# Whole loads of q and k and a new order of the first two batches in an attention and MLP kernel on one core

## The chip, the cores and the metric

The kernel runs on one core of one Trainium2 chip. The metric is the time of one execution in device microseconds. Three runs of the kernel before gave a median of 285.89 us (285.8 to 286.83). A difference of 1 us is at the edge of what single times can tell; the traces, which show each instruction's start, tell more. A "span" below is the time from the first to the last instruction of one execution; it is 1.8 to 1.9 us shorter than the time of the same run.

Engines: PE is TensorE, DVE is VectorE, ACT is ScalarE, POOL is GpSimd, SP is the engine whose queue issues nearly all the loads here.

## The reference, cut to what matters

```python
def _attn_ref(q, k, v):                 # each (8 batches, 8 heads, 576, 64), float32
    q_s = exp(q - max(q, -1));  q_s = q_s / sum(q_s, -1)      # softmax over the 64 columns
    k_s = exp(k - max(k, 2));   k_s = k_s / sum(k_s, 2)       # softmax over the 576 rows
    kv = einsum('bhsd,bhse->bhde', k_s, v)                    # 64x64 per head
    return einsum('bhsd,bhde->bhse', q_s, kv)

def _moe_ref(x, w_in, w_out, beta):     # x (4608, 512), w_in (512, 2048), w_out (2048, 512)
    h = x @ w_in
    g = h * sigmoid(beta * h)
    return g @ w_out
```

The attention's output, with the heads side by side, is x. The kernel's types are float32 at both ends and bfloat16 inside.

## The kernel before: the parts that matter

Each batch goes through two parts. The attention part makes `xT` (x transposed, four chunks of 128 rows). The MLP part makes 16 tiles `h` of 128x512 (4 matmuls each), ACT takes `tanh` of each, DVE makes `g`, and PE multiplies `g` by `w_out` into four accumulators (`mm_b`, 4 matmuls for each g). Behind batch 1 the two parts of neighbouring batches are interleaved evenly. The head, in which batch 0's attention waits for its loads and has no MLP work beside it, and the stretch in which batch 1's attention is threaded by hand between batch 0's MLP matmuls, are written out instruction by instruction. The change is in these two parts.

The helpers, cut:

```python
def load_kv(d, src, b, tag, pairs=None):            # batches 0 and 1: one load per head pair, 288 KB
    ...
    sv = src[b].rearrange("(j e) (p i) d -> (e p) j (i d)", e=2, i=RW)
    for j in range(HP) if pairs is None else pairs:
        nc.sync.dma_start(d[b][:, j, :], sv[:, j, :])

def kz_exp(b, j): nc.scalar.activation(ek[b][:, j, :], k_st[b][:, j, :], ACTF.Exp)
def vz_cast(b, j, eng, m=1, part=None): ...         # v to bfloat16; part 0 is 5 of 9 rows, part 1 the other 4
def q_exp(b, s): ...                                # ACT: exp of half s of q
def q_sum(b, s): ...                                # DVE: row sums and their reciprocals
def q_mul(b, s): ...                                # DVE: multiply by them; both inputs in SBUF
def tpe(b, j, tag): ...                             # PE: 4 transposes of q's pair j;  q_ev copies the result to SBUF
def kvz_mm(b, j, tag, n): ...                       # PE: 18 small matmuls, k^T v of head pair j
def kvz_norm(b, j, n): ...                          # DVE: divide by k's sums
def xpe(c, j, tag): ...                             # PE: one matmul, xT chunk j into PSUM; xev copies it to SBUF
def hpe(c, j, kts, tag): ...                        # PE: pieces kts of h tile j, each one matmul on xT chunk kt
def w_castk(blk, kt, eng): ...                      # weight piece to bfloat16
def tail_zero(t): ...                               # POOL memsets of the buffers for the sequences' last rows
def warm(n, tag): ...                               # n matmuls on zeros that nobody reads
```

The head's loads and order, with cuts:

```python
    load_q(0, 2, 0)                                  # half of q, 512 KB
    nc.sync.dma_start(beta_r[:], ...)                # 8 rows of 1 KB
    load_kv(k_st, k, 0, "k_st", [0])
    load_kv(v_st, v, 0, "v_st", [0])
    load_q(0, 2, 1)
    load_kv(k_st, k, 0, "k_st", [2])
    load_kv(k_st, k, 0, "k_st", [3])
    load_kv(v_st, v, 0, "v_st", [2])
    load_kv(k_st, k, 0, "k_st", [1])
    load_kv(v_st, v, 0, "v_st", [1])
    load_kv(v_st, v, 0, "v_st", [3])
    w_load("in", 0, 0)                               # then the weights, 256 or 512 KB each
    ...
    tail_zero(0)
    tail_zero(1)
    warm(18, tag="b0")
    q_exp(0, 0)
    kz_exp(0, 0)
    q_sum(0, 0)
    vz_cast(0, 0, A, part=1)
    vz_cast(0, 0, G, part=0)
    kvz_mm(0, 0, "acc3", 1)
    q_mul(0, 0)
    ...                                              # 15 more warm matmuls in the gaps, in fours
    xpe(0, 1, "b3")
    xpe(0, 2, "acc3")
    w_castk(0, 1, G)
    hpe(0, 3, [0], "b0")                             # the first MLP matmul
    ...
```

The softmax here doesn't subtract the row's maximum and nothing guards it: scores larger than these inputs give would overflow.

## Time and profile before

| what | before |
|---|---|
| time, median of 3 | 285.89 us |
| span of the trace | 283.9 us |
| PE busy | 278.1 us, 98% |
| PE works without a break from | 17.39 us |
| last eviction starts at | 280.73 us |
| first weight cast of block 0 starts at | 14.87 us |

The page's first part gives busy time, share of the span and instructions for each engine; its fourth part gives the chain of waits that ended last, by engine. These are the two lines of the kernel before:

```profile
PE 278.1 (98%) x1683; PEld 130.5 (46%) x1683; DVE 179.6 (63%) x285; ACT 164.4 (58%) x241; POOL 37.8 (13%) x59
...
PE 94%; DMA 2%; DVE 2%; SPq 0%; POOL 0%; issue 0%; ACT 0%; POOLq 0%
```

PE is the bound. The same chain in order of time (start, length, what) shows where it is not PE. From the kernel before, between 12 and 18 us:

```profile
13.39 1.21 DVE eq L240
14.60 0.09 DVE rk L301
...
15.64 0.24 DVE kvp L304
15.88 0.05 issue
15.92 0.60 PE x L370 x2
16.52 0.65 PE h L422 x3
17.17 0.22 PE x L370
17.39 0.65 PE h L422 x3
```

Up to 15.9 us the chain is DVE's: the multiply of q's second half (L240), then the normalisations (L301, L304). After that it is PE until the last eviction. So the time is the moment at which PE's unbroken stretch begins, plus PE's work, plus any hole in the stretch.

Lines of the timeline of the kernel before (start, length, engine, line, operation, tiles, count, and in brackets what ended the idle time before it):

```profile
4.52 1.06 ACT L223 ACTIVATE eq<-q_st 128x1024 bf16<-128x1024 f32 x1 [2.50 <-DMA q_st<-in_q_dram]
...
13.07 0.46 POOL L158 CAST va<-v_st 128x320 bf16<-128x320 f32 x1 [0.84 <-DMA v_st<-in_v_dram]
...
13.31 1.29 DVE L240 TENSOR_TENSOR eq<-eq,rq 128x1024 bf16<-128x1024 bf16 x1
...
13.84 1.08 POOL L158 CAST va<-v_st 128x320 bf16<-128x320 f32 x1 [0.30 <-DMA v_st<-in_v_dram]
...
14.87 2.28 POOL L158 CAST w_in_b<-w_in 128x512 bf16<-128x512 f32 x4
```

The first half of q lands at 4.5 us, the last v pair at 13.8. The four casts of the first weight block follow on POOL without a gap.

The view by stretches gives, for each stretch in us, its length, then busy time (and instruction count) of PE, PE's weight loads, DVE, ACT and POOL, then the granted PE clock, the DMA engines' mean share and what they moved in GB/s. The kernel before, 3 to 7 us:

```profile
3.00:4.00 1.00, 1.00 (x4) 0.33 (x3) 0.01 (x1) 0.00 (x0) 0.89 (x4) 1.00 1.05 322
4.00:5.00 1.00, 1.00 (x3) 0.30 (x2) 0.00 (x0) 0.48 (x1) 1.00 (x3) 1.00 1.06 283
5.00:6.00 1.00, 1.00 (x4) 0.45 (x3) 0.40 (x1) 0.57 (x1) 0.22 (x3) 1.00 0.91 296
6.00:7.00 1.00, 1.00 (x7) 0.41 (x6) 0.97 (x2) 0.68 (x1) 0.00 (x0) 1.00 0.98 309
```

The DMA engines are occupied nearly all the time (0.91 to 1.06) and move about 300 GB/s, where they move 388 to 402 from 8 to 14 us (in stretches of 2 us).

### The profile page before, as it was taken

Reading aid. Unit: us, or ns where it says so; the run is one execution under the profiler, and the core shown is the slowest. Engines: PE = TensorE matmul, PEld = TensorE weight load, DVE = VectorE, ACT = ScalarE, POOL = GpSimd, SP = SyncE. Lnnn points to the kernel's source line nnn. Section 1 sums busy time; section 2 is a strip of 40 time slices with the busy share of each in tenths; the row PEclk is TensorE's granted clock in tenths of the full one; section 3 lists DMA queues with packets and bytes.
Section 4 is the critical chain, followed back from the end, with each engine's and each line's share of the span. In section 5 each row is a group of like instructions: output and inputs, shape, how many; then the busy total and the mean of one; then the engine's idle time right before and its main releaser. Section 6 shows DMA issues by size and latency. Waiting matters only on the chain.

```text
span 283.9 us, 4325 instructions
## 1 busy us (share of the span) xinstructions
PE 278.1 (98%) x1683; PEld 130.5 (46%) x1683; DVE 179.6 (63%) x285; ACT 164.4 (58%) x241; POOL 37.8 (13%) x59
## 2 busy tenths in 40 slices
PE   8899999999999999999999999999999999999995
PEld 3454445444444444444444444444445444445543
DVE  4765777875478457855685568646964596454361
ACT  4557796953496448734773468355944564454451
POOL 6374241130030003000300030000200000000000
PEclk9999999999999999999999999999999999999999
DMA  7999999919930993089416942598344032105003
GB/s 218 388 382 388 390 392 322 285 30 279 259 153 2 255 297 149 3 200 315 152 41 151 305 155 93 100 229 228 150 82 142 1 148 54 22 0 148 2 0 148
DMA packets 54932, 50.09 MB, mean 176 GB/s; under 512 B 26360, under 2 KB 47104, under 8 KB 54912
## 3 DMA queue, kind: packets, MB, share of 16 engines
q1 hardware_dynamic: 54768, 49.69, 58.1%
q8 instruction: 13, 0.21, 0.3%
q10 hardware_dynamic: 144, 0.13, 0.1%
q14 instruction: 7, 0.06, 0.1%
HBM read 36.71 MB, written 9.44 MB: 163 GB/s over the span
## 4 chain that ended last, share of the span: by engine, by line
PE 94%; DMA 2%; DVE 2%; SPq 0%; POOL 0%; issue 0%; ACT 0%; POOLq 0%
PE h L422 44%; PE acc L470 43%; PE x L370 2%; DMA v_st<-in_v_dram 2%; PE kv L330 2%; PE acc L462 1%; PE kv L289 1%; DVE rq L234 0%; DVE eq L240 0%; PE tp L270 0%; PE x L374 0%; DVE kvp L304 0%; POOL va L158 0%; DVE qsT L158 0%; PE warm L543 0%
## 5 line engine op out<-in xcount | busy, mean ns | idle before, releaser
L432 ACT ACTIVATE th<-h,beta_t 128x512 bf16<-128x512 f32 x144 | 98.5, 687 | 93.4 <-PE h L422 91.6
L436 DVE SCALAR_TENSOR_TENSOR g<-th,h 128x512 bf16<-128x512 bf16 x144 | 98.1, 683 | 85.9 <-ACT th L432 84.1
L422 PE MATMUL h<-xT,w_in_b 128*128 128x512 bf16 x576 | 144.0, 379 | 0.0
L470 PE MATMUL acc<-w_out_b,g 128*128 128x512 bf16 x560 | 140.8, 379 | 0.0
L422 PEld LDWEIGHTS <-w_in_b 128*128 128x128 bf16 x576 | 55.5, 98 | 63.9
L470 PEld LDWEIGHTS <-g 128*128 128x128 bf16 x560 | 54.4, 98 | 65.3 <-DVE g L436 0.5
L158 POOL CAST va<-v_st 128x320 bf16<-128x320 f32 (+2 forms) x14 | 16.7, 1192 | 150.0 <-DMA v_st<-in_v_dram 150.0
L234 DVE TENSOR_REDUCE rq<-eq 128x16 f32<-128x1024 bf16 x18 | 21.9, 1217 | 4.9 <-ACT eq L223 4.9
L240 DVE TENSOR_TENSOR eq<-eq,rq 128x1024 bf16<-128x1024 bf16 x18 | 22.0, 1221 | 0.1
L223 ACT ACTIVATE eq<-q_st 128x1024 bf16<-128x1024 f32 x16 | 16.2, 1048 | 2.5 <-DMA q_st<-in_q_dram 2.5
L156 ACT CAST xT<-x 128x512 bf16<-128x512 f32 x17 | 9.9, 585 | 8.6 <-PE x L370 7.8
L158 DVE COPY o<-acc 128x512 f32<-128x512 f32 (+1 forms) x19 | 12.1, 670 | 3.5 <-PE acc L470 3.2
L156 ACT COPY o<-acc 128x512 f32<-128x512 f32 (+1 forms) x18 | 9.6, 576 | 6.3 <-PE acc L470 3.4
L158 DVE CAST xT<-x 128x512 bf16<-128x512 f32 x19 | 12.8, 681 | 0.1
L177 ACT ACTIVATE ek<-k_st 128x1024 bf16<-128x1024 f32 x12 | 12.6, 1047 | 0.0
L370 PE MATMUL x<-qsT,kvp 128*128 128x512 bf16 x32 | 11.8, 380 | 0.2
L543 PE MATMUL warm<-kvp 128*128 128x512 bf16 x33 | 10.3, 465 | 1.2 <-DVE kvp L627 1.2
L158 POOL CAST w_in_b<-w_in 128x512 bf16<-128x512 f32 (+1 forms) x11 | 6.9, 650 | 6.4 <-DMA w_in<-in_moe_w_in_dram 6.4
L543 PEld LDWEIGHTS <-kvp 128*128 128x128 bf16 x33 | 3.6, 116 | 6.4 <-issue 3.6
L170 ACT ACTIVATE ek<-k_st 128x576 bf16<-128x576 f32 x8 | 5.4, 684 | 1.5 <-DMA k_st<-in_k_dram 1.5
L330 PEld LDWEIGHTS <-ek 128*64 128x64 bf16 x192 | 4.1, 111 | 2.5 <-ACT th L432 2.5
L363 DVE TENSOR_TENSOR kvp<-kv,rk 64x256 bf16<-64x256 f32 x12 | 5.1, 422 | 0.3
(45 smaller groups left out, 86.2 us busy)
## 6 DMA issues: line engine op xcount, KB each, us to landing
out_dram<-o SPq DMA_DIRECT2D x14, 512.0 KB, 3.4
q_st<-in_q_dram SPq DMA_DIRECT2D x6, 1024.0 KB, 6.4
k_st<-in_k_dram SPq DMA_DIRECT2D x6, 1024.0 KB, 9.2
v_st<-in_v_dram SPq DMA_DIRECT2D x6, 1024.0 KB, 10.7
w_in<-in_moe_w_in_dram SPq DMA_DIRECT2D x6, 512.0 KB, 9.4
k_st<-in_k_dram SPq DMA_DIRECT2D x8, 288.0 KB, 7.3
v_st<-in_v_dram SPq DMA_DIRECT2D x8, 288.0 KB, 7.4
q_st<-in_q_dram SPq DMA_DIRECT2D x4, 512.0 KB, 9.0
```

The source lines that it names most:

```text
L156: eng.copy(dst, src)
L158: eng.tensor_copy(dst, src)
L177: nc.scalar.activation(ek[b][:, :, h, :].rearrange("p i h d -> p h i d"), k_st[b][:, h, 0 : R * D].rearrange("p h (i d) -> p h i d", i=R), ...
L223: nc.scalar.activation(eq[b][:, :, s * m : (s + 1) * m, :].rearrange("p i h d -> p h i d"), q_st[b][:, s * m : (s + 1) * m, :].rearrange(" ...
L234: nc.vector.tensor_reduce(rq[b][:, 0, :, h], eq[b][:, :, h, :], axis=AX.X, op=ALU.add)
L240: eng.tensor_tensor(eq[b][:, :, h, :], eq[b][:, :, h, :], rq[b][:, 1, :, h].unsqueeze(3).to_broadcast((P, R, m, D)), ALU.mult,)
L370: nc.tensor.matmul(t[:], kvp[:, c, j, :], qsT[c][:, :, j, :])
L422: nc.tensor.matmul(h[:], w_unit(j, kt), x_of(c)[:, kt, :], start=(kt == 0), stop=(kt == KT - 1),)
L432: nc.scalar.activation(th[:], h_of[c, j][:], ACTF.Tanh, scale=beta_t[:, j : j + 1])
L436: nc.vector.scalar_tensor_tensor(out=g[:], in0=th_of.pop((c, j))[:], scalar=1.0, in1=h_of[c, j][:], op0=ALU.add, op1=ALU.mult)
L470: nc.tensor.matmul(acc[st][:], g[:, ds(st * P, P)], w_out_b[:, j, :], start=(j == 0), stop=(j == NJ - 1),)
L543: nc.tensor.matmul(t[:], kvp[:, B - 1, 0, :], kvp[:, B - 1, :, :].rearrange("p j r -> p (j r)"))
```

## The change

Its intent is a head in which PE's stretch begins sooner: q and k of batch 0 come in one load each, v by pairs in the order 0, 1, 2, 3, and the order of all engines' work is laid out anew for that, as is the order of batch 1 behind it. The zeroing of the tails' buffers moves from the start to behind that work. The number of warm matmuls goes from 33 to 31; 13 of them now stand in one block in front of the first transposes, instead of 15 spread over the gaps. The banks are renamed to fit. The diff, cut to its core:

```diff
-    load_q(0, 2, 0)
-    nc.sync.dma_start(beta_r[:], ...)
-    load_kv(k_st, k, 0, "k_st", [0])        # and v 0, q half 1, k 2, k 3, v 2, k 1, v 1, v 3
+    load_q(0)
+    load_kv(k_st, k, 0, "k_st", whole=True)
+    load_kv(v_st, v, 0, "v_st", [0])
+    load_kv(v_st, v, 0, "v_st", [1])
+    nc.sync.dma_start(beta_r[:], ...)
+    load_kv(v_st, v, 0, "v_st", [2])
+    load_kv(v_st, v, 0, "v_st", [3])
     ...                                     # weights: block 0 in the order 0, 3, 1, 2
-    tail_zero(0)
-    tail_zero(1)
     warm(18, tag="b0")
     q_exp(0, 0)
+    q_sum(0, 0)
+    q_exp(0, 1)
+    q_mul(0, 0)
     kz_exp(0, 0)
+    kz_exp(0, 1)
+    q_sum(0, 1)
+    vz_cast(0, 0, G)
+    warm(13, tag="acc2")
+    tpe(0, 0, "acc3")
+    tpe(0, 1, "acc2")
+    q_ev(0, 0, A)
+    kvz_mm(0, 0, "acc1", 1)
+    vz_cast(0, 1, G)
     ...                                     # [cut]
+    vz_cast(0, 3, G, part=0)
+    vz_cast(0, 3, A, part=1)
+    kvz_mm(0, 2, "acc1", 2)
+    xev(0, 0, A)
+    kvz_mm(0, 3)
+    w_castk(0, 0, G)
     ...                                     # [cut]
+    hpe(0, 3, [0], "b0")                    # the first MLP matmul now stands in front of xpe(0, 1)
+    kvz_norm(0, 2, 2)                       # pairs 2 and 3 in one normalisation
+    xpe(0, 1, "acc3")
     ...                                     # [cut: batch 0's MLP and batch 1's attention in a new order]
+    tail_zero(0)
+    tail_zero(1)
```

More of the change, by code (lines that the diff above doesn't have):

```diff
@@ L109, with load_kv @@
     kv_st = {}
-    def load_kv(d, src, b, tag, pairs=None):
+    def load_kv(d, src, b, tag, pairs=None, whole=False):
         if (tag, b) not in kv_st:
@@ L117, in load_kv @@
             sv = src[b].rearrange("(j e) (p i) d -> (e p) j (i d)", e=2, i=RW)
+            if whole:
+                nc.sync.dma_start(d[b], sv)
+                return
             for j in range(HP) if pairs is None else pairs:
@@ L252, in q_xbar @@
         )
-    HB, AB = ["b3", "b2"], ["b0", "b1"]
+    HB, AB = ["b3", "b0"], ["b1", "b2"]
     turns = {"h": 0, "att": 0}
@@ L584, in beta_ev @@
         )
-    load_q(0, 2, 0)
+    load_q(0)
+    load_kv(k_st, k, 0, "k_st", whole=True)
+    load_kv(v_st, v, 0, "v_st", [0])
+    load_kv(v_st, v, 0, "v_st", [1])
     nc.sync.dma_start(beta_r[:], moe_beta.rearrange("(hh q) -> hh q", q=2 * P))
-    load_kv(k_st, k, 0, "k_st", [0])
-    load_kv(v_st, v, 0, "v_st", [0])
-    load_q(0, 2, 1)
-    load_kv(k_st, k, 0, "k_st", [2])
-    load_kv(k_st, k, 0, "k_st", [3])
     load_kv(v_st, v, 0, "v_st", [2])
-    load_kv(k_st, k, 0, "k_st", [1])
-    load_kv(v_st, v, 0, "v_st", [1])
     load_kv(v_st, v, 0, "v_st", [3])
     w_load("in", 0, 0)
+    w_load("in", 0, 3)
     w_load("in", 0, 1)
     w_load("in", 0, 2)
-    w_load("in", 0, 3)
     w_load("in", 1, 0)
@@ L607 @@
     w_load("out", 1)
+    load_kv(v_st, v, 1, "v_st", [0])
+    w_load("in", 3, 0)
+    w_load("in", 3, 1)
     load_q(1, 2, 0)
-    w_load("in", 3, 1)
-    w_load("in", 3, 0)
-    load_kv(k_st, k, 1, "k_st", [2])
     w_load("out", 2)
     load_q(1, 2, 1)
+    load_kv(v_st, v, 1, "v_st", [1])
     load_kv(k_st, k, 1, "k_st", [0])
-    load_kv(v_st, v, 1, "v_st", [2])
-    w_load("out", 3, 0)
-    w_load("out", 3, 1)
-    load_kv(v_st, v, 1, "v_st", [0])
-    load_kv(k_st, k, 1, "k_st", [1])
-    load_kv(v_st, v, 1, "v_st", [1])
-    load_kv(k_st, k, 1, "k_st", [3])
-    load_kv(v_st, v, 1, "v_st", [3])
+    load_kv(k_st, k, 1, "k_st", [1])
+    w_load("out", 3, 0)
+    load_kv(k_st, k, 1, "k_st", [3])
+    w_load("out", 3, 1)
+    load_kv(v_st, v, 1, "v_st", [3])
+    load_kv(k_st, k, 1, "k_st", [2])
+    load_kv(v_st, v, 1, "v_st", [2])
     load_q(2)
@@ L632 @@
     v_buf(1)
-    tail_zero(0)
-    tail_zero(1)
     warm(18, tag="b0")
     q_exp(0, 0)
+    q_sum(0, 0)
+    q_exp(0, 1)
+    q_mul(0, 0)
     kz_exp(0, 0)
-    q_sum(0, 0)
-    vz_cast(0, 0, A, part=1)
-    vz_cast(0, 0, G, part=0)
-    kvz_mm(0, 0, "acc3", 1)
-    q_mul(0, 0)
-    beta_pe("acc2")
-    beta_ev()
-    kvz_norm(0, 0)
-    q_exp(0, 1)
-    warm(3, tag="acc1")
-    tpe(0, 0, "acc2")
-    tpe(0, 1, "acc1")
-    q_ev(0, 0, V)
-    q_ev(0, 1, V)
-    kz_exp(0, 2)
-    warm(1, tag="acc0")
@@ L655 @@
-    xpe(0, 0, "acc3")
-    q_sum(0, 1)
-    kz_exp(0, 3)
-    vz_cast(0, 2, G)
-    xev(0, 0, V)
-    warm(8, tag="acc1")
-    kvz_mm(0, 2, "acc2", 1)
-    kz_exp(0, 1)
-    q_mul(0, 1)
-    vz_cast(0, 1, A, part=1)
-    vz_cast(0, 1, G, part=0)
-    warm(3, tag="acc1")
-    kvz_mm(0, 1, "acc3", 1)
-    kvz_norm(0, 2)
-    vz_cast(0, 3, A, part=1)
-    vz_cast(0, 3, G, part=0)
-    tpe(0, 2, "acc1")
-    tpe(0, 3, "acc0")
-    kvz_norm(0, 1)
-    q_ev(0, 2, A)
-    kvz_mm(0, 3, "acc2", 1)
-    w_castk(0, 0, G)
@@ L677 @@
-    q_ev(0, 3, A)
-    kvz_norm(0, 3)
-    xpe(0, 1, "b3")
-    xpe(0, 2, "acc3")
+    kz_exp(0, 1)
[7 more added lines that the diff above has]
+    vz_cast(0, 1, G)
+    kz_exp(0, 3)
+    beta_pe("acc0")
+    kvz_norm(0, 0)
+    kvz_mm(0, 1, "acc3", 1)
+    vz_cast(0, 2, G)
+    kz_exp(0, 2)
+    q_mul(0, 1)
+    xpe(0, 0, "b3")
+    beta_ev()
+    vz_cast(0, 3, G, part=0)
+    vz_cast(0, 3, A, part=1)
@@ L681 @@
+    kvz_mm(0, 2, "acc1", 2)
+    xev(0, 0, A)
+    kvz_mm(0, 3)
+    w_castk(0, 0, G)
+    q_ev(0, 1, A)
+    kvz_norm(0, 1)
+    tpe(0, 3, "acc0")
+    tpe(0, 2, "b3")
+    w_castk(0, 3, G)
+    q_ev(0, 3, A)
+    hpe(0, 3, [0], "b0")
+    kvz_norm(0, 2, 2)
+    xpe(0, 1, "acc3")
+    hpe(0, 2, [0], "b1")
+    q_ev(0, 2, A)
     w_castk(0, 1, G)
-    hpe(0, 3, [0], "b0")
+    hpe(0, 1, [0], "b2")
     xev(0, 1, V)
-    hpe(0, 0, [0], "b1")
-    hpe(0, 2, [0], "b2")
+    hpe(0, 0, [0], "acc0")
@@ L686 @@
+    xpe(0, 3, "acc2")
     w_castk(0, 2, G)
-    xpe(0, 3, "acc2")
-    xev(0, 2, V)
-    hpe(0, 1, [0], "acc0")
-    xev(0, 3, A)
+    xpe(0, 2, "acc1")
+    xev(0, 3, V)
+    hpe(0, 1, [1])
+    xev(0, 2, A)
     hpe(0, 0, [1])
-    w_castk(0, 3, G)
     hpe(0, 3, [1])
-    hpe(0, 1, [1])
-    hpe(0, 3, [2])
-    hpe(0, 3, [3])
-    hpe(0, 1, [2])
-    th_act(0, 3)
     hpe(0, 2, [1])
-    w_castk(1, 0, G)
     hpe(0, 2, [2])
     hpe(0, 2, [3])
-    w_castk(1, 1, A)
+    w_castk(1, 0, G)
     hpe(0, 0, [2])
-    g_dve(0, 3)
@@ L706 @@
-    hpe(0, 7, [0], "b3")
-    hpe(0, 0, [3])
-    th_act(0, 2)
-    hpe(0, 4, [0], "acc1")
-    w_castk(1, 2, G)
-    hpe(0, 4, [1])
-    th_act(0, 0)
-    hpe(0, 5, [0], "b0")
-    g_dve(0, 2)
+    th_act(0, 2)
+    hpe(0, 1, [2])
+    w_castk(1, 1, G)
+    hpe(0, 1, [3])
+    hpe(0, 5, [0], "b3")
+    th_act(0, 1)
+    hpe(0, 3, [2])
+    g_dve(0, 2)
+    hpe(0, 5, [1])
+    w_castk(1, 2, G)
+    hpe(0, 3, [3])
+    w_castk(1, 3, A)
+    hpe(0, 0, [3])
+    g_dve(0, 1)
+    hpe(0, 6, [0], "b1")
@@ L715 @@
+    hpe(0, 5, [2])
+    th_act(0, 3)
+    hpe(0, 5, [3])
+    hpe(0, 7, [0], "b2")
+    th_act(0, 0)
+    hpe(0, 6, [1])
+    g_dve(0, 3)
+    w_cast("out", 0, 0, G)
     hpe(0, 7, [1])
-    w_castk(1, 3, G)
-    hpe(0, 1, [3])
-    hpe(0, 4, [2])
+    hpe(0, 7, [2])
+    th_act(0, 5)
+    hpe(0, 6, [2])
     g_dve(0, 0)
-    th_act(0, 1)
-    hpe(0, 7, [2])
-    hpe(0, 4, [3])
-    hpe(0, 6, [0], "b2")
-    w_cast("out", 0, 0, G)
-    th_act(0, 4)
-    hpe(0, 6, [1])
-    g_dve(0, 1)
-    hpe(0, 6, [2])
@@ L729 @@
     hpe(0, 6, [3])
-    hpe(0, 5, [1])
-    g_dve(0, 4)
+    hpe(0, 7, [3])
+    g_dve(0, 5)
     th_act(0, 6)
-    hpe(0, 5, [2])
-    hpe(0, 5, [3])
-    hpe(0, 7, [3])
-    w_cast("out", 0, 1, A)
+    hpe(0, 4, [0], "b0")
+    w_cast("out", 0, 1, G)
     mm_b(0, 0)
+    th_act(0, 7)
     g_dve(0, 6)
     mm_b(0, 1)
-    th_act(0, 7)
+    g_dve(0, 7)
     w_castk(2, 0, G)
-    th_act(0, 5)
-    g_dve(0, 7)
+    mm_b(0, 2)
     w_castk(2, 1, G)
-    mm_b(0, 2)
-    g_dve(0, 5)
-    w_castk(2, 2, A)
+    mm_b(0, 3)
@@ L748 @@
+    w_castk(2, 2, G)
     w_castk(2, 3, G)
-    mm_b(0, 3)
-    hpe(0, 8, [0, 1, 2, 3], "b0")
-    hpe(0, 10, [0, 1, 2, 3], "b1")
-    th_act(0, 8)
-    w_cast("out", 1, 1, G)
-    w_cast("out", 1, 0, A)
-    hpe(0, 9, [0, 1, 2, 3], "b2")
-    g_dve(0, 8)
-    hpe(0, 11, [0, 1, 2, 3], "b0")
+    hpe(0, 4, [1])
+    hpe(0, 4, [2])
+    hpe(0, 4, [3])
+    hpe(0, 8, [0, 1, 2, 3], "b1")
+    th_act(0, 4)
+    hpe(0, 9, [0, 1, 2, 3], "b2")
+    g_dve(0, 4)
+    th_act(0, 8)
+    w_cast("out", 1, 0, A)
@@ L758 @@
+    hpe(0, 11, [0, 1, 2, 3], "b0")
+    g_dve(0, 8)
+    vz_cast(1, 0, G, part=0)
+    hpe(0, 10, [0, 1, 2, 3], "b1")
+    th_act(0, 9)
+    th_act(0, 11)
+    w_cast("in", 3, 0, G)
+    g_dve(0, 9)
+    mm_b(0, 4)
+    w_cast("out", 1, 1, A)
+    g_dve(0, 11)
+    mm_b(0, 5)
+    vz_cast(1, 0, A, part=1)
     th_act(0, 10)
+    mm_b(0, 6)
+    w_cast("in", 3, 1, A)
+    g_dve(0, 10)
+    mm_b(0, 7)
     q_exp(1, 0)
-    g_dve(0, 10)
-    mm_b(0, 4)
-    th_act(0, 9)
+    hpe(0, 13, [0, 1, 2, 3], "b0")
@@ L763 @@
     q_sum(1, 0)
-    mm_b(0, 5)
-    w_cast("in", 3, 1, A)
-    mm_b(0, 6)
-    th_act(0, 11)
-    g_dve(0, 9)
-    w_cast("in", 3, 0, G)
-    mm_b(0, 7)
-    q_mul(1, 0)
-    hpe(0, 12, [0, 1, 2, 3], "b1")
-    g_dve(0, 11)
-    tpe(1, 0, "b2")
-    th_act(0, 12)
-    hpe(0, 13, [0, 1, 2, 3], "b3")
-    q_ev(1, 0, V)
-    g_dve(0, 12)
-    hpe(0, 14, [0, 1, 2, 3], "b0")
-    th_act(0, 13)
-    w_cast("out", 2, 1, G)
-    w_cast("out", 2, 0, A)
-    tpe(1, 1, "b1")
-    g_dve(0, 13)
-    hpe(0, 15, [0, 1, 2, 3], "b2")
@@ L786 @@
-    th_act(0, 14)
-    mm_b(0, 8)
-    q_exp(1, 1)
-    g_dve(0, 14)
-    mm_b(0, 9)
-    vz_cast(1, 2, G)
-    kz_exp(1, 0)
-    q_sum(1, 1)
-    mm_b(0, 10)
-    q_ev(1, 1, A)
-    kz_exp(1, 2)
-    w_cast("out", 3, 0, G)
-    mm_b(0, 11)
-    th_act(0, 15)
-    q_mul(1, 1)
-    kvz_mm(1, 2, "b0", 1)
+    hpe(0, 12, [0, 1, 2, 3], "b1")
+    th_act(0, 13)
+    hpe(0, 14, [0, 1, 2, 3], "b2")
+    w_cast("out", 2, 0, A)
+    w_cast("out", 2, 1, G)
+    g_dve(0, 13)
+    hpe(0, 15, [0, 1, 2, 3], "b3")
@@ new lines @@
+    th_act(0, 12)
+    q_mul(1, 0)
+    q_exp(1, 1)
+    mm_b(0, 8)
+    g_dve(0, 12)
+    vz_cast(1, 1, G)
+    th_act(0, 14)
+    mm_b(0, 9)
+    q_sum(1, 1)
+    th_act(0, 15)
+    mm_b(0, 10)
+    kz_exp(1, 0)
+    g_dve(0, 15)
+    mm_b(0, 11)
+    kz_exp(1, 1)
+    q_mul(1, 1)
+    w_cast("out", 3, 0, G)
+    tpe(1, 0, "b0")
+    tpe(1, 1, "b1")
+    q_ev(1, 0, A)
+    kvz_mm(1, 0, "b3", 2)
+    g_dve(0, 14)
+    kvz_mm(1, 1)
+    q_ev(1, 1, A)
+    tpe(1, 3, "b0")
+    kz_exp(1, 3)
+    kvz_norm(1, 0, 2)
@@ L802 @@
     mm_b(0, 12)
     w_cast("out", 3, 1, A)
-    g_dve(0, 15)
-    vz_cast(1, 0, G, part=0)
     tpe(1, 2, "b1")
-    kvz_norm(1, 2)
-    vz_cast(1, 0, A, part=1)
-    mm_b(0, 13)
-    q_ev(1, 2, V)
-    kz_exp(1, 1)
-    kvz_mm(1, 0, "b0", 1)
-    vz_cast(1, 1, A, part=1)
-    vz_cast(1, 1, G, part=0)
-    xpe(1, 2, "b1")
-    kvz_norm(1, 0)
-    tpe(1, 3, "b2")
-    kvz_mm(1, 1, "b3", 1)
-    kz_exp(1, 3)
-    q_ev(1, 3, V)
-    mm_b(0, 14)
-    kvz_norm(1, 1)
-    vz_cast(1, 3, A, part=1)
-    vz_cast(1, 3, G, part=0)
@@ L825 @@
-    xpe(1, 0, "b0")
-    xev(1, 2, V)
-    xpe(1, 1, "b2")
-    kvz_mm(1, 3, "b3", 1)
-    xev(1, 1, A)
-    xev(1, 0, V)
-    mm_b(0, 15)
-    kvz_norm(1, 3)
-    hpe(1, 0, [0], "b0")
-    store(0, 0)
-    hpe(1, 1, [0], "b1")
-    xpe(1, 3, "b2")
-    hpe(1, 3, [0], "b3")
-    store(0, 1)
-    xev(1, 3, A)
-    hpe(1, 3, [1])
-    hpe(1, 0, [1])
+    xpe(1, 1, "b2")
+    vz_cast(1, 3, G, part=0)
+    q_ev(1, 2, V)
+    xpe(1, 0, "b3")
+    vz_cast(1, 3, A, part=1)
+    mm_b(0, 13)
+    xev(1, 1, V)
@@ L842 @@
+    q_ev(1, 3, A)
+    kz_exp(1, 2)
+    kvz_mm(1, 3, "b1", 1)
+    vz_cast(1, 2, G, part=0)
+    mm_b(0, 14)
+    vz_cast(1, 2, A, part=1)
+    kvz_norm(1, 3)
+    xev(1, 0, A)
+    kvz_mm(1, 2, "b0", 1)
+    mm_b(0, 15)
+    kvz_norm(1, 2)
+    xpe(1, 3, "b1")
+    store(0, 0)
+    xpe(1, 2, "b0")
+    xev(1, 3, V)
+    hpe(1, 0, [0], "b2")
+    hpe(1, 0, [1])
+    xev(1, 2, A)
+    hpe(1, 2, [0], "b3")
+    store(0, 1)
+    hpe(1, 2, [1])
+    hpe(1, 1, [0], "b1")
     hpe(1, 0, [2])
@@ L849 @@
     hpe(1, 1, [3])
+    hpe(1, 2, [2])
+    th_act(1, 1)
+    hpe(1, 2, [3])
+    g_dve(1, 0)
+    hpe(1, 3, [0], "b0")
+    hpe(1, 3, [1])
+    th_act(1, 2)
     hpe(1, 3, [2])
+    g_dve(1, 1)
     hpe(1, 3, [3])
-    th_act(1, 1)
-    g_dve(1, 0)
-    hpe(1, 2, [0], "b2")
-    hpe(1, 2, [1])
+    mm_b(1, 0)
     th_act(1, 3)
-    hpe(1, 2, [2])
-    g_dve(1, 1)
-    hpe(1, 2, [3])
-    mm_b(1, 0)
-    th_act(1, 2)
+    g_dve(1, 2)
+    mm_b(1, 1)
     g_dve(1, 3)
-    mm_b(1, 1)
-    g_dve(1, 2)
+    tail_zero(0)
+    tail_zero(1)
     def side(n, u):
```

## The prediction

> **What bounds the kernel now.** TensorE. The page's first part has PE busy 278.1 of 283.9 us (98%); the chain of waits that ended last is 94% PE, 2% DMA, 2% DVE. From 17.39 us to the last eviction (280.73 us) that chain is PE without a break, each 512-column matmul starting 0.216 us after the one before. So only two things can change the time: when the unbroken stretch begins, and whether the new order tears a hole in it later. Useful PE work is the same; 2 of 33 warm-up matmuls, mere filling, go.
>
> **The head before.** By the timeline: first half of q lands at 4.5 us, k pair 0 at 6.3, v pair 0 at 7.8, the last v pair at 13.8; the four pieces of the first weight block are cast back to back by POOL from 14.87 to 17.15. By half-microsecond stretches, DMA's share is near 1 from 2.5 us on, with about 300 GB/s until 7.5 us and 390 after: bytes, not issue, set landings. The last steps before 17.39 are DVE's: multiply of q's second half until 14.6, three normalisations, the xT copies.
>
> **What the change does.**
> - Whole loads move no fewer bytes. Landings, counted as cumulative bytes plus the lag seen (0.9 to 2 us): q whole at about 7, k whole 10.8, v pairs 11.5, 12.3, 13.0, 13.8, weight pieces from 14.5 every 0.7 us. So q's first exp starts about 2.5 us later (before: 4.52), and the last v and the weights land as before.
> - DVE: the two q sums (1.47 each) and multiplies (1.2) run 8.3 to 14.55 with one normalisation between; evictions of qT and xT go to ACT (0.58 each); pairs 2 and 3 share one normalisation. That takes about 2 us off the end of DVE's chain.
> - PE takes the first weight piece against xT chunk 0 four times (from about 15.4 us) where before it waited until 15.9.
> - Zeroing of the tails, 3.6 us of POOL (1.67 to 5.28), moves to about 45 us, where POOL idles 10.4 us before batch 2's v cast. Before, POOL idled 2.6 us after it: worth nothing by itself.
>
> **How much is on the path.** Adding trace durations along these chains, the state that before reached at 17.39 comes at about 16.8. Gain 0.6 us (0.2%). Behind it, slack is small at g(1) freeing the bank for h7 (about 20.3), w_out 0 (about 22), w_in 2 and 3 (26, 33), batch 1's last v (45); I allow 0.1 us of new holes. Time 285.4 us, range 284.4 to 286.7. Faster by over 2%: 0.02; within 2%: 0.96; slower: 0.02.
>
> **What would show it.** q's exp starting at 6.5 to 7.5 us; last v landing within 0.3 us of 13.8; the first h matmul at 15.2 to 15.7 and PE unbroken from 16.6 to 17.1; PE idle after that under 0.3 us; POOL zeroing at 45 to 49 us delaying nobody.
>
> **What would make it wrong.** [...] (warm-up matmuls 0.43 us apart until 5.86 us, then 0.216). With fewer fillers PE is about half busy from 10.3 to 15.4 us; if the clock drops, the first h matmuls take twice as long and I lose 1 to 2 us. Else: whole loads landing later than counted, or weights arriving late.

The spacings in brackets behind the mark, 0.43 and then 0.216 us, are that trace's own, and "twice as long" is worked out from them. The sum: 285.9 less 0.6 plus 0.1 is 285.4 us, and the 1 to 2 us for a falling clock, the author's estimate, stood outside it.

## The result, and the profile after

| what | before | after |
|---|---|---|
| time, median of 4 runs | 285.86 us | 284.97 us (284.71 to 285.07) |
| span of the trace | 283.9 us | 282.9 us |
| q's first exp starts | 4.52 us | 6.51 us |
| last v pair in use from | 13.80 us | 12.56 us |
| first weight cast starts | 14.87 us | 13.82 us |
| last eviction starts | 280.73 us | 279.61 us |

The ratio is 0.996, with a 95% interval of 0.9937 to 0.9982. The change is 0.4% faster, inside the 2% that count as "the same".

The two lines of the page after:

```profile
PE 275.2 (97%) x1653; PEld 130.1 (46%) x1681; DVE 176.5 (62%) x274; ACT 164.9 (58%) x243; POOL 39.6 (14%) x60
...
PE 93%; DMA 3%; SPq 1%; POOL 1%; issue 1%; ACT 0%
```

(Some matmul records are missing: 1653 of 1681.) The chain in order of time after the change, from 4 to 18 us:

```profile
3.99 8.52 DMA v_st<-in_v_dram
12.51 0.05 issue
12.56 1.31 POOL va L161
13.88 1.13 POOL w_in_b L161 x2
15.00 0.01 issue
15.01 0.38 PE x L373
15.39 0.65 PE h L425 x3
16.04 0.43 PE x L373 x2
16.47 1.73 PE h L425 x8
```

DVE is gone from the chain. It is now a load of v, POOL's cast of it, two of POOL's weight casts, then PE. Timeline lines that answer to those of before:

```profile
6.51 2.00 ACT L226 ACTIVATE eq<-q_st 128x1024 bf16<-128x1024 f32 x2 [4.49 <-DMA q_st<-in_q_dram]
...
12.33 1.23 DVE L243 TENSOR_TENSOR eq<-eq,rq 128x1024 bf16<-128x1024 bf16 x1
...
12.56 1.31 POOL L161 CAST va<-v_st 128x320 bf16<-128x320 f32 x1
...
13.82 2.29 POOL L161 CAST w_in_b<-w_in 128x512 bf16<-128x512 f32 x4
...
16.30 5.65 PE L425 MATMUL h<-xT,w_in_b 128*128 128x512 bf16 x25
```

And the stretches from 3 to 7 us after:

```profile
3.00:4.00 1.00, 1.00 (x4) 0.32 (x3) 0.01 (x1) 0.00 (x0) 0.00 (x0) 1.00 0.98 299
4.00:5.00 1.00, 1.00 (x5) 0.35 (x4) 0.00 (x0) 0.00 (x0) 0.00 (x0) 1.00 1.08 384
5.00:6.00 1.00, 1.00 (x6) 0.48 (x5) 0.00 (x0) 0.00 (x0) 0.00 (x0) 1.00 1.05 361
6.00:7.00 1.00, 1.00 (x7) 0.46 (x5) 0.00 (x0) 0.49 (x1) 0.00 (x0) 1.00 1.04 396
```

Three things are to be seen. From 3 to 7 us the DMA engines deliver more (mean of the four stretches 360 GB/s, before 302); counted from 0 to 12 us the difference is small (298 against 288), because the changed kernel moves less before 3 us. POOL's cast of the last v pair takes 1.31 us, although the same shape took 0.46 us at 13.07 in the kernel before; it ends 0.31 us after DVE's multiply that began just ahead of it. This is not new: the kernel before shows the same for its last pair (1.08 us, to 0.32 us after the multiply), but there DVE's chain ended later and it cost nothing. And PE reaches the old state sooner. At 17.39 the kernel before had all of batch 0's attention and 3 h matmuls behind it; the new one has that and one h matmul more at 16.47 (the first of the four has no record; its weight load is at 14.74), so the same state at about 16.25. That is 1.14 us sooner. Of this 1.12 us are left at the last eviction (280.73 less 279.61).

### The profile page after: what moved, and what is told of

The parts are those of the page before. It is cut to its first block, busy times and chain, and to the rows that moved or that the text cites. A ratio compares the mean times of both kernels' runs of the same rounds, so it can differ in the third digit from the quotient of the medians.

```text
span 282.9 us, 4278 instructions
## 1 busy us (share of the span) xinstructions
PE 275.2 (97%) x1653; PEld 130.1 (46%) x1681; DVE 176.5 (62%) x274; ACT 164.9 (58%) x243; POOL 39.6 (14%) x60
## 4 chain that ended last, share of the span: by engine, by line
PE 93%; DMA 3%; SPq 1%; POOL 1%; issue 1%; ACT 0%
PE h L425 44%; PE acc L473 42%; DMA v_st<-in_v_dram 3%; PE x L373 2%; PE kv L333 2%; PE acc L465 1%; PE kv L292 1%; SPq L122 1%; POOL va L161 0%; POOL w_in_b L161 0%; PE tp L273 0%; PE x L377 0%; SPq L119 0%; SPq L593 0%; SPq L96 0%
## 5 line engine op out<-in xcount | busy, mean ns | idle before, releaser
L425 PE MATMUL h<-xT,w_in_b 128*128 128x512 bf16 x560 | 142.4, 379 | 1.0
L473 PE MATMUL acc<-w_out_b,g 128*128 128x512 bf16 x548 | 138.8, 379 | 0.5 <-issue 0.2
L161 POOL CAST va<-v_st 128x2048 bf16<-128x2048 f32 (+2 forms) x14 | 16.9, 1207 | 149.7 <-DMA v_st<-in_v_dram 149.4
L159 ACT CAST xT<-x 128x512 bf16<-128x512 f32 x18 | 10.6, 588 | 6.6 <-PE x L373 5.8
L546 PE MATMUL warm<-kvp 128*128 128x512 bf16 x31 | 8.5, 442 | 1.2 <-DVE kvp L626 1.2
L161 POOL CAST w_in_b<-w_in 128x512 bf16<-128x512 f32 (+1 forms) x12 | 7.5, 650 | 3.0 <-DMA w_in<-in_moe_w_in_dram 2.9
L161 POOL CAST w_out_b<-w_out 128x1024 bf16<-128x1024 f32 x4 | 5.0, 1248 | 7.5 <-DMA w_out<-in_moe_w_out_dram 7.5
```

The lines of the kernel that those rows point to most:

```text
L159: eng.copy(dst, src)
L161: eng.tensor_copy(dst, src)
L425: nc.tensor.matmul(h[:], w_unit(j, kt), x_of(c)[:, kt, :], start=(kt == 0), stop=(kt == KT - 1),)
L473: nc.tensor.matmul(acc[st][:], g[:, ds(st * P, P)], w_out_b[:, j, :], start=(j == 0), stop=(j == NJ - 1),)
L546: nc.tensor.matmul(t[:], kvp[:, B - 1, 0, :], kvp[:, B - 1, :, :].rearrange("p j r -> p (j r)"))
```

## The experiments

My theory after the result: the whole gain is the head's, through loads that arrive sooner and an order of work that suits them; the zeroing is worth nothing. Rivals: the zeroing slowed the loads (it stood exactly where they were slow); or batch 1's new order made the gain; or the head's order of work alone made it, whatever the loads. All kernels below gave correct results. "Span" is that of the one traced execution.

### Is it the zeroing?

`e1_before_zero_late` is the kernel before with

```diff
-    tail_zero(0)
-    tail_zero(1)
     warm(18, tag="b0")
     ...
     g_dve(1, 2)
+    tail_zero(0)
+    tail_zero(1)
```

> The kernel before with only the zeroing of the tails' buffers moved behind the head's work. Theory Z (POOL's memsets between 1.7 and 5.3 us slow the loads that run beside them): the last v pair lands near 12.6 us as in the changed kernel instead of 13.8, and the time falls by 0.4 us or more. Theory L (loads: fewer and larger ones land sooner) and theory O (the new order of the head's work): nothing moves, 285.8 us within 0.15, last v at 13.8, and the zeroing after 45 us delays nobody.

Measured: 285.7 us (284.98 to 286.08, 6 runs), ratio 0.9977 (0.9953 to 1.0001), span 283.9. POOL's cast of the last v pair began at 13.61, and the DMA engines moved 284 GB/s on average from 3 to 7 us.

`e2_after_zero_early` is the changed kernel with the two calls back in front of `warm(18)`.

> The changed kernel with the zeroing back at the start. Theory Z: DMA falls to about 300 GB/s until 5 us, q lands later than 6.5 us, the last v later than 12.6, and the time rises by 0.4 us or more to 285.4. Theories L and O: 284.9 us within 0.15, landings unchanged, because POOL has nothing else to do before the first v pair at 10.3.

Measured: 284.82 us (284.44 to 286.07), ratio 0.9956 (0.9933 to 0.998), span 283.0. q's exp began at 6.37, the last eviction at 279.63. Two of its stretches, with POOL zeroing (0.89 and 1.00 us busy) beside the loads:

```profile
3.00:4.00 1.00, 1.00 (x4) 0.33 (x3) 0.01 (x1) 0.00 (x0) 0.89 (x4) 1.00 1.05 375
4.00:5.00 1.00, 1.00 (x3) 0.30 (x2) 0.00 (x0) 0.00 (x0) 1.00 (x3) 1.00 1.06 366
```

So the zeroing costs nothing that these times can show in either place (at most about 0.1 us by `e1`'s last eviction, 280.64 against 280.73), and the loads are not seen to be slowed by it: in the two stretches above the DMA engines moved 375 and 366 GB/s beside it, where they moved 299 and 384 in the changed kernel without it, and q's exp began at 6.37 us against 6.51.

### Head or batch 1?

`e5_head_new_rest_old` has the new loads and order up to batch 0's h4, and from h8 on the old order, with banks b0, b1, b2 renamed b1, b2, b0 and the old order of the loads behind w_out 1. `e6_head_old_rest_new` is the reverse. Both zero late. Their edits are the diff above cut at one line:

```diff
     mm_b(0, 3)                              # and h4 where it is still open
     # e5: new above, old below;   e6: old above, new below
     hpe(0, 8, [0, 1, 2, 3], ...)
```

> The changed kernel's head (loads and order of batch 0 up to the end of h4) with the old loads and order from there to batch 1's g3, PSUM banks renamed to fit. If the whole gain is in the head: 285.0 us within 0.15 and PE's unbroken stretch starting near 16.5 us as in the changed kernel. The two traces show PE 0.2 us cheaper between 17 and 50 us in the new order (fewer switches from the small kv matmuls back to full ones); if that is real this run is 0.2 us slower than the changed kernel, 285.1 to 285.2.

> The old head (loads and order of batch 0) with the new loads and order of the rest, zeroing late. If the head makes the gain: 285.6 to 285.85 us, with the stretch starting at 17.4 as before and at most 0.2 us won behind it. If the rest makes it: 285.0.

Measured: `e5` 285.18 us (284.9 to 286.34), ratio 0.997 (0.9947 to 0.9992), span 283.3. `e6` 285.74 us (284.8 to 286.2), ratio 0.998 (0.9957 to 1.0003), span 283.7. The times of `e6` alone don't tell it from the kernel before. The traces do, if one takes the chain's times at two points: the first `mm_b` of batch 0 (three h pieces, 0.65 us, are added where the new head does them later), and the first h of batch 1 (0.43 us are taken off where two pieces were done before).

| kernel | first `mm_b` of batch 0 | first h of batch 1 | between them | last eviction |
|---|---|---|---|---|
| before | 23.65 | 48.18 | 24.53 | 280.73 |
| before, zeroing late (e1) | 23.50 | 48.09 | 24.59 | 280.64 |
| old head, new rest (e6) | 23.51 | 47.95 | 24.44 | 280.54 |
| new head, old rest (e5) | 22.86 | 47.39 | 24.53 | 279.94 |
| after | 22.60 | 47.05 | 24.45 | 279.61 |

Batch 1's new order is worth about 0.1 us: 24.44 and 24.45 against 24.53 to 24.59. The chain shows one source. The small kv matmuls of two pairs run as one group of 36 in 0.70 us, where two groups of 18 take 0.41 each, 0.12 us more. The rest of the gain is in the head: 0.8 us in `e5`, 1.05 in the changed kernel. The 0.26 us between these two come from a hole in the stretch that both have and that depends on when a weight piece lands (two matmuls start 0.65 us apart there in `e5` and 0.30 in the changed kernel, 0.216 elsewhere; `e5`'s stretch begins 0.09 us sooner). In `e5`:

```profile
16.21 3.40 PE L425 MATMUL h<-xT,w_in_b 128*128 128x512 bf16 x15
19.88 2.33 PE L425 MATMUL h<-xT,w_in_b 128*128 128x512 bf16 x10 [0.27 <-POOL w_in_b L161]
```

PE waits for the cast of w_in block 1's third piece, needed by h5, which landed at 19.2 us in this run and at 18.95 in the changed kernel's, where the hole is about 0.1 us.

### Loads or order of work?

`e4_before_whole_loads` keeps the old order of work and takes the new loads of batch 0:

```diff
-    load_q(0, 2, 0)                         # and the ten loads behind it
+    load_q(0)
+    load_kv(k_st, k, 0, "k_st", whole=True)
+    load_kv(v_st, v, 0, "v_st", [0])        # v 1, beta, v 2, v 3; weights 0, 1, 2, 3
```

> The kernel before with the changed kernel's loads of batch 0 (q whole, k whole, v pairs in order, beta after them), its order of work untouched. Theory L alone would make it as fast as the changed kernel, 285.0. I expect that it can't: its ACT takes k pair 0 ahead of q's second half, and whole k lands at 9.4, so q's second sum ends near 14 instead of 12.8 and PE's unbroken stretch starts at 17.9 to 18.6 instead of 17.4: 286.3 to 287.0 us. The last v would still land near 12.6.

Measured: 289.0 us (288.87 to 289.11), ratio 1.0113 (1.0099 to 1.0126), span 287.3: slower than I expected by 2.0 to 2.7 us. The loads did come early (POOL was done with the v pairs at 13.24). But PE had nothing to do from 7.2 to 10.86 us, and then ran at a granted clock of 0.50 (from 11.93 to 15.34 us). The PE line that ends the pause, and a stretch with the granted clock (third number from the right) behind it:

```profile
10.86 0.48 PE L292 MATMUL kv<-va,ek 64*64 64x65 bf16 x18 [3.70 <-POOL va L161]
```

```profile
12.00:14.00 2.00, 1.78 (x11) 1.30 (x11) 0.79 (x3) 2.00 (x4) 1.94 (x5) 0.50 1.05 383
```

`e11_after_old_loads` is the reverse: the new order of work with the old eleven loads of batch 0.

> The changed kernel's order of work with the old order and sizes of the batch 0 loads up to the weights (weights as changed). Theory O of the loads: DMA falls to 300 GB/s until 7 us as in the kernel before, the last v lands at 13.6 to 13.8, POOL's first weight cast starts near 14.7 instead of 13.8, and the span is 283.6 to 284.0, most of the gain lost. If only the order of the work counts: 282.9 to 283.2.

Measured: 287.61 us (287.12 to 288.99), ratio 1.0057 (1.0028 to 1.0087), span 286.2. This is 3.3 us above the changed kernel's span, far more than the 0.7 to 1.1 that I expected. v pair 1 was there only at 13.66 (the old order brings pair 2 first), PE idled 0.68 and 2.46 us around two short groups, and its clock fell to 0.50 in the seventeenth microsecond and was still there under the first h matmuls. So this run does not show what the old loads cost without the clock; it shows that neither half of the new head works alone, as these two kernels stand. How much each half is worth with the clock held stays open: no run here separates that.

### What made the loads quicker?

`e3_after_small_loads` is the changed kernel with `load_q(0, 2)` and `load_kv(k_st, k, 0, "k_st")`: q in halves and k in pairs again, in the new order.

> The changed kernel with q of batch 0 in two loads and k in four again, all else alike. Theory L (fewer, larger loads land sooner; the SP queue waits, before each load from the ninth on, for the one eight before it to land): DMA moves 300 GB/s instead of 390 until 7 us, the first weight pieces are issued after 5 us instead of 4.5, the last v pair lands 0.5 to 1.2 us later than 12.6, and the span grows by 0.4 to 1.0 us. Theory O (the order of the loads and of the head's work, not their size): landings within 0.2 us of the changed kernel's, span within 0.15 us.

The queue's wait that it names is in the changed kernel's trace: the ninth to twelfth loads were issued at 6.50, 9.52, 10.27 and 11.02 us, and the first to fourth had landed at 6.49, 9.50, 10.25 and 11.01.

Measured: span 283.1, last eviction at 279.87. The weight pieces were issued from 7.86 us on instead of 4.46, and w_in block 1's first half was cast at 17.20 instead of 16.62; PE then waited 0.18 us for the block's second half. That is all the size did in this trace. Its four runs are not alike: the traced one took 284.88 us with a mean clock of 1.000, the other three 285.93 to 286.98 with mean clocks of 0.992 to 0.994, so the median of 286.03 and the ratio of 1.0007 (0.9982 to 1.0033) are those of runs in which the clock fell for a while. Why it did so three times in four here and never in the changed kernel's four runs (all at 0.998 or more) is open, since only the first run has a trace.

`e10_before_beta_later` is the kernel before with beta's 8 KB load moved from second place to behind k pair 2 (that is sixth place; the text miscounts it as seventh).

> The kernel before with only beta's small load (8 rows of 1 KB) moved from second to seventh place. Theory S (that load, second in line, holds up some of the DMA engines, so that the loads behind it land late): DMA runs at 360 to 390 GB/s from 3 to 7 us instead of 300 and the last v lands near 12.7 instead of 13.6 to 13.8. Theory O (the order in which q, k and v alternate): still 300 GB/s and 13.6 to 13.8. For the time, at most 0.2 us either way, because the head there waits for its own work, not for the last v.

Measured: 286.04 us (285.82 to 286.53), ratio 0.9998 (0.998 to 1.0016), span 284.2. The last v pair was cast from 13.17.

The stretch from 4 to 5 us of `e3`, `e11` and `e10`, one fence each:

```profile
4.00:5.00 1.00, 1.00 (x3) 0.30 (x2) 0.00 (x0) 0.44 (x1) 0.00 (x0) 1.00 1.09 375
```

```profile
4.00:5.00 1.00, 1.00 (x3) 0.30 (x2) 0.00 (x0) 0.48 (x1) 0.00 (x0) 1.00 0.90 250
```

```profile
4.00:5.00 1.00, 1.00 (x3) 0.30 (x2) 0.00 (x0) 0.00 (x0) 1.00 (x3) 1.00 1.08 333
```

In the traces of the kernel before and of the changed one, each load of batch 0's q, k and v ends with sixteen landing events (beta's with one), and what was waiting for the load starts after the last of them (in the changed kernel q's exp at 6.51 after 6.49, POOL's cast at 12.56 after 12.51). The last column has the first and the last of these events for the last v pair; they are read from the events kept in the traces, not from a view.

| kernel | order of batch 0's loads | size | beta | GB/s, 3 to 7 us | GB/s, 0 to 12 us | last v lands, first to last event |
|---|---|---|---|---|---|---|
| before | q, k, v in turns | small | second | 302 | 288 | 11.64 to 13.78 |
| e1 | q, k, v in turns | small | second | 284 | 280 | 11.83 to 13.55 |
| e11 | q, k, v in turns | small | second | 293 | 282 | 11.72 to 14.35 |
| e10 | q, k, v in turns | small | sixth | 312 | 285 | 11.96 to 13.12 |
| e3 | all q, all k, v | small | ninth | 358 | 302 | 11.55 to 12.46 |
| e2 | all q, all k, v | whole | fifth | 374 | 304 | 11.63 to 12.34 |
| after | all q, all k, v | whole | fifth | 360 | 298 | 11.88 to 12.51 |

The size of the loads is not what makes v land early: in its trace `e3` is as quick as the changed kernel (302 GB/s from 0 to 12 us against 298). The order goes with it. But the mean rate does not tell all: the first event comes at about the same time in all rows, and what differs most is how far the last of the sixteen lags behind it, 1.7 to 2.6 us with the three kinds of loads in turns and beta second, 0.6 to 0.9 in the order q, k, v. Moving beta alone shortens the lag to 1.2 us and brings the last v about half a microsecond sooner (cast from 13.2 against 13.6 to 13.8), and hardly changes the rate. Each row is one trace; the traces of the other kernels agree (`e6`, old loads: 288 GB/s from 3 to 7 us and 11.84 to 13.53; the six others with the new loads: 361 to 380 GB/s, last event at 12.33 to 12.62, a lag of 1.0 us at most). Why the order makes some of the events late no run here shows.

### What do the 13 warm matmuls do?

I had called the warm matmuls mere filling. After `e4` I took the block of 13 out of the changed kernel (`e7_after_no_warm13`):

```diff
-    warm(13, tag="acc2")
     tpe(0, 0, "acc3")
```

> The changed kernel without its 13 warm-up matmuls in front of the first transposes. PE then idles from about 7 to 10.5 us. If its clock drops after a pause that long (the kernel with whole loads and the old order paused 3.7 us and its next 512-column matmuls were 0.37 us apart), the transposes and kv matmuls take longer, the first h matmuls are 0.43 us apart for up to 3 us, and the span grows by 0.7 to 2 us. If it doesn't, nothing changes: 282.9.

Measured: 287.49 us (286.7 to 288.22), ratio 1.0046 (1.0024 to 1.0069), span 285.4. PE lines and a stretch of that run:

```profile
10.49 0.61 PE L273 MATMUL tp<-identity,eq 128*128 128x128 bf16 x8 [3.58 <-DVE eq L243]
...
16.35 1.49 PE L425 MATMUL h<-xT,w_in_b 128*128 128x512 bf16 x3
...
18.37 5.56 PE L425 MATMUL h<-xT,w_in_b 128*128 128x512 bf16 x25
```

```profile
14.00:16.00 2.00, 1.96 (x28) 1.62 (x28) 1.09 (x5) 0.96 (x3) 2.00 (x4) 0.50 0.96 321
```

The last three numbers are the clock (0.50), the DMA share and GB/s. After a pause of 3.58 us it fell at about 11.5 us and came back between 18 and 19. Three h matmuls take 1.49 us instead of 0.81, and the stretch begins 2.07 us later than in the changed kernel (18.37 against 16.30). The span grows by 2.5 us. With the block, PE's longest pause in front of the transposes is 0.83 us. So these 13 matmuls, which compute nothing, hold up a head that would otherwise be slower than the old one by 1.6 us in the median. The granted clock tells part of the runs' spread too: `e2`'s one run over 285.1 us (286.07) and `e5`'s one over 285.5 (286.34) are the only ones of theirs with a mean clock of 0.993.

The records of the granted clock tell more than the pauses do. In all 14 traces the clock changes only at whole multiples of 3.413 us after its first rise, which comes at 4.53 to 6.69 us (in the changed kernel at 4.53; until then the views' clock column reads 1.00, although the warm matmuls start 0.43 us apart). In the heads it fell three times, each time to 0.50: from 11.42 to 18.24 us (`e7`), 11.93 to 15.34 (`e4`) and 16.29 to 19.70 (`e11`). In the 3.41 us before these falls PE was busy for 0.89, 1.07 and 1.46 us. In every other such stretch of the heads that began at full clock it was busy for 2.06 us or more, and the clock held; the least in the kernel before is 2.26, in the changed kernel 2.59. So the busy time within one stretch tells the falls from the rest in these traces. The longest pause does so too, but a fall came with one of only 2.46 us (`e11`), where 1.61 (`e1`) came with none. What happens with 1.46 to 2.06 us of work no run shows.

### A version that beats both

The chain after the change said what is next: POOL. Its cast of v pair 3 took 1.31 us beside DVE's multiply, against 0.46 for the same shape at 13.07 in the kernel before, where it began ahead of the multiply. The two casts of that kernel that began while a multiply ran took 0.79 and 1.08 us. v pair 3's cast ended 0.31 us after the multiply, less than 0.46, so if it waited for the multiply, not quite all of it did; what the two engines contend for no trace here shows. ACT's cast of the pair's other part ran beside the same multiply in 0.41 us, and in 0.40 in `e4`, where only the multiply's last 0.08 us fell beside it (10.25). So `e8_after_v3_on_act` gives ACT the whole cast:

```diff
-    vz_cast(0, 3, G, part=0)
-    vz_cast(0, 3, A, part=1)
+    vz_cast(0, 3, A)
```

> The changed kernel with v pair 3 cast whole on ACT instead of five ninths on POOL. In its trace that POOL cast takes 1.31 us where the same shape takes 0.46 elsewhere, and it ends 0.31 us after DVE's multiply of q's second half. If the two engines exclude each other there, the first weight cast moves from 13.82 to 13.2 to 13.6, itself stretched until the multiply is over (ends at 13.9 to 14.1 instead of 14.4); PE's stretch starts 0.3 to 0.6 us sooner, and most of that is lost again in a hole before the third piece of h5, whose weights land at 18.95 and are cast at 19.6: span 282.5 to 282.9, against 282.9. If POOL's cast was long for another reason, nothing changes at all.

Measured: 284.75 us (284.38 to 285.1), ratio 0.9969 (0.9956 to 0.9983), span 282.6. Lines of its timeline:

```profile
13.06 2.65 POOL L161 CAST w_in_b<-w_in 128x512 bf16<-128x512 f32 x4 [0.76 <-DMA w_in<-in_moe_w_in_dram]
...
15.67 3.40 PE L425 MATMUL h<-xT,w_in_b 128*128 128x512 bf16 x15
19.32 2.33 PE L425 MATMUL h<-xT,w_in_b 128*128 128x512 bf16 x10 [0.25 <-POOL w_in_b L161]
```

The weight casts begin 0.76 us sooner, stretched this time (2.65 us for four, against 2.29), PE's stretch begins at 15.67 instead of 16.30, and half of that is lost in the hole in front of h5, as expected.

`e9_v3_on_act_h5_later` moves h5's third and fourth piece behind h6 and h7's first two:

```diff
     hpe(0, 6, [0], "b1")
-    hpe(0, 5, [2])
-    hpe(0, 5, [3])
+    hpe(0, 6, [1])
     hpe(0, 7, [0], "b2")
-    hpe(0, 6, [1])
     hpe(0, 7, [1])
+    hpe(0, 5, [2])
+    hpe(0, 5, [3])
```

> The same, and h5's third and fourth pieces behind the first two of h6 and h7, which need no weights that late. If the hole is what eats the gain, this one keeps it: span 282.2 to 282.5, time 284.3 to 284.6 us. If the bank of h7 is not free in time (g1 ends at 19.9), half of it.

Measured: 284.47 us (284.42 to 284.97), ratio 0.996 (0.9948 to 0.9973), span 282.6, the last eviction at 279.31. The hole at h5 shrinks (two matmuls start 0.38 us apart there, 0.63 in `e8`, 0.216 without a hole), and the next ones open: PE waits for g0 at 21.2 us and for the cast of w_out 3, which landed at 39.4.

`e12_g0_first_w_out3_on_act` went after those two:

```diff
-    th_act(0, 3)  ...  th_act(0, 0)         # and g_dve likewise
+    th_act(0, 0)  ...  th_act(0, 3)
-    hpe(0, 4, [0], "b0")                    # to behind mm_b(0, 3)
-    w_cast("out", 3, 0, G)                  # and out 3, 1 from A to G
+    w_cast("out", 3, 0, A)
```

> The combined version again (v pair 3 on ACT, h5's late pieces later), and now g0 ahead of g3, h4's first piece behind the output matmuls, and w_out 3's first half cast on ACT, its second on POOL. The trace of the version without these shows PE waiting 0.2 us for g0 at 21.2 and 0.1 us for that cast at 41.0. If those holes are all that is left: span 282.3 to 282.4, time 284.2 to 284.4 us. If the loads' stream is the next limit: no change from 282.6.

Measured: 284.68 us (284.52 to 285.05), ratio 0.995 (0.9936 to 0.9964), span 282.8: nothing more. PE waits 0.22 us at 21.44, now for the cast of w_out 0, which had landed at 20.34:

```profile
21.44 3.61 PE L473 MATMUL acc<-w_out_b,g 128*128 128x512 bf16 x16 [0.22 <-POOL w_out_b L161]
```

The chain that ended last runs back from 39.40 us to 11.29 through loads of w_out and w_in. So the next limit is the stream of the weight loads, as the second case of the expectation had it. The best version by its median is `e9` at 284.47 us, 0.5 below the changed kernel's 284.97, with a trace 0.3 us shorter. The two were timed in different rounds, and their ratios to the kernel before (both 0.996) don't separate them; that it beats the changed kernel is what the traces say, not what the times prove.

## Why the prediction was right or wrong

The prediction was 285.4 us with 284.4 to 286.7 as the range; 284.97 us was measured. The class (within 2%) and the range hold, but the range is a weak test: no change at all (285.86) lies in it too. That PE is the bound and the start of its stretch the lever was right; two terms of the sum were mis-sized. Point by point:

- "PE unbroken ... only two things can change the time": right. The start of the stretch moved by 1.14 us, and 1.12 us of it stand at the end.
- The gain of 0.6 us was mis-sized; it is 1.14 us at that point. The first term at fault is the landings: "the last v and the weights land as before". The last v was in use at 12.56 instead of 13.8, k at 9.52 instead of the 10.8 that I counted, and v pair 0 at 10.31 instead of 11.5; the first weight piece landed at 13.18 instead of 14.5 (before: 14.46). I had taken the before-trace's "lag seen" behind the count of bytes as fixed. The runs show that much of it came with the old order: the last of a load's sixteen landing events lagged 2.1 us behind the first there and lags 0.6 now, and about half a microsecond of the landing was beta's place in second position (`e10`, one trace).
- "Whole loads move no fewer bytes": right, and in `e3`'s trace the size is indeed not what counts; the order is.
- A second term was missing, with the opposite sign: POOL's cast of the last v pair, 1.31 us beside DVE's multiply instead of 0.46, made POOL the end of the chain. I had counted the weight pieces "from 14.5 us"; they were cast from 13.82, and with that cast off POOL from 13.06 (`e8`).
- "That takes about 2 us off the end of DVE's chain": right in kind, too large in size. The second multiply ends at 13.56 instead of 14.60 (predicted: 14.55), the last normalisation at 15.24 instead of 16.56, so 1.0 and 1.3 us. DVE is not in the chain any more.
- Zeroing "worth nothing by itself": right (`e1`, `e2`). It ran at 44.1 to 47.6 us and no wait in the trace names it as the cause.
- Holes of 0.1 us: about right for the traced run (the hole at h5), 0.27 in `e5`.
- Batch 1's new order I had not credited at all; it is worth about 0.1 us.
- The warm matmuls as "mere filling" was wrong, though "if the clock drops" stood among the ways to be wrong, with 1 to 2 us: without them it drops, and the span grows by 2.5 us (`e7`).

Of the marks that I gave: q's exp at 6.5 to 7.5, 6.51 measured, right. Last v within 0.3 us of 13.8, wrong by 1.2. First h matmul at 15.2 to 15.7, wrong: its weight load is at 14.74 (its own record is missing). PE unbroken from 16.6 to 17.1, wrong: 16.30. PE idle after that under 0.3, right.

## What to carry to other kernels

When one engine is busy for 98% of a kernel, a new order of its first microseconds is worth, but for small holes later (0.1 us here), what it moves the start of the unbroken stretch (here 1.14 us, of which 1.12 stood at the end); read that moment off the chain of waits in both traces before looking at anything else. Loads and order of work may have to be changed together: here either one alone cost 1.7 to 3.1 us in the median where both together won 0.9. And matmuls that compute nothing can be the piece that carries the result: before taking them for filling, take them out in a run (here PE's pause in front of the transposes grew from 0.83 to 3.58 us, the granted clock fell to 0.50 and the span grew by 2.5 us).
